# Attention beside a Mish layer on one core: strips and w1 pieces in the buffers of the gated rows, eleven power buffers in place of nine, and a new written order

## The chip, the core and the metric

The kernel runs on one core of a Trainium2 chip. The metric is the device time of one execution in microseconds (us), the median of several. Before the change it is 684.99 us (684.69 to 685.27 over three runs). One further execution was profiled; all rows of the profile below come from it.

The engines are called as the profile calls them: PE (matmul), PEld (its weight loads, which overlap it), DVE (VectorE), ACT (ScalarE), POOL (GpSimd) and SP (SyncE, whose queue issues nearly all DMAs).

## What is computed

```python
B, S, D = 1, 2048, 640            # of A and B; F = 1536
...
def _A_ref(x, wqkv, wo):
    B, S, D = x.shape
    H = 32; Dh = D // H
    qkv = (lambda x, *d: x.transpose(*d))((x @ wqkv).reshape(B, S, 3, H, Dh), 2, 0, 3, 1, 4)
    q, k, v = qkv[0], qkv[1], qkv[2]
    scale = Dh ** -0.5
    scores = jnp.einsum("bhqd,bhkd->bhqk", q, k) * scale
    p = _softmax(scores, axis=-1)
    o = jnp.einsum("bhqk,bhkd->bhqd", p, v)
    return (lambda x, *d: x.transpose(*d))(o, 0, 2, 1, 3).reshape(B, S, D) @ wo

def _B_ref(x, w1, b1, w2):
    h = jnp.einsum("bsd,df->bsf", x, w1) + b1
    sp = jnp.log1p(jnp.exp(-jnp.abs(h))) + jnp.where(h > 0, h, jnp.zeros_like(h))
    act = h * jnp.tanh(sp)
    return jnp.einsum("bsf,fd->bsd", act, w2)

x = A_x
g = _sigmoid((x * gate_w).sum(-1, keepdims=True))
a = _A_ref(x, A_wqkv, A_wo)
b = _B_ref(x, B_w1, B_b1, B_w2)
return g * a + (1 - g) * b
```

## The kernel before

**Tiling of the attention.** The 32 heads go in 8 sets of four, the 2048 queries in 4 columns of 512: 32 *groups* G of four heads and 512 queries. The keys of a group go in 16 *tiles* j of 128. One tile of one head is a *unit*: a score matmul (line 1074, contraction over 32 rows, so four heads can use four row groups of PE), 128 keys by 512 queries, into one PSUM bank of 512 f32. Banks 0 to 6 rotate, bank 7 is the accumulator `acc`. There are 32 x 16 x 4 = 2048 units.

**Two ways to the exponential.** For 345 of the 512 tiles ACT computes it (line 1092, one, two or three banks at a time) into a ring E of 18 slots. For the other 167 tiles DVE writes an integer approximation of a power of two (line 587), one instruction for each unit, into a buffer T of 4 x 512 bf16. Such a tile is then completed by POOL: two 64-bit integer additions over T (line 617) make shifted copies, in other buffers T or in place. Mostly the three versions go into the sum one by one (three P·V products, two of them with V scaled by a ratio, `VD`). Where a tile is taken with `two` = 1, DVE adds two versions first (line 641, 2048 elements), and two P·V products are enough. The buffers T are named by number, nine of them, 4 KB of each partition.

**P·V.** `emit_pv` (line 1109) multiplies four heads at once: four matmuls of 21 output columns side by side, 512 wide, into `acc`. The 21st column of V is ones and gives the denominator. When a group's last product is in, DVE transposes and divides (lines 1138 to 1152), and SP stores the result to DRAM.

**Chains.** All other products are *chains* (line 664): K, Q and V from x, h = x·w1, Mish·w2, and attention rows times wo. A piece of a chain is one contraction step: four matmuls of 32 output columns side by side, 512, 320, 240 or 81 wide. Q and K are made strip by strip (128 of their columns), each strip of weights loaded into one of two buffers for Q and two for K (`ws0_0`, `ws0_1`, `ws1_0`, `ws1_1`, `load_strip`); w1 comes in 24 pieces into two buffers (`w1t0`, `w1t1`, `load_w1`). Late in the kernel the attention rows come back transposed into two buffers `od0` and `od1` (`load_o`) to be multiplied by wo and gated. Mish itself is done by ACT in two instructions of 12288 elements (line 872), each between two loads of an activation table.

**The written order.** No scheduler moves anything: the string `ORDER` at the top of the file lists every step, and each engine and queue runs its own steps in that order, waiting on semaphores where data or a buffer is not ready. The letters: `S n,k` n score matmuls into banks from k on for ACT; `x n` one exp over n banks; `d G,k,two` takes a tile for the powers with buffer T number k; `D G,j,r,k` one score matmul of such a tile into bank k; `y n` the n-th waiting DVE instruction; `p n,k` the n-th waiting POOL addition, into buffer T number k (-1: in place); `V j,i` one P·V product of four matmuls; `C i,k` begins chain i in bank k and `F` emits a piece of it; `H` is four matmuls with zero weights (line 1124), which keep PE occupied; `m` is a Mish; `q`, `k`, `l`, `b`, `o` issue loads on SP.

Below, a *column group* is four matmuls side by side, as in `V`, `F` or `H`, and a *score run* is a stretch of score matmuls (`S`, `D`) with no column group between them.

Of the kernel before, what the change touches and what calls it, by code (L numbers as in the profile page):

```python
# [9 lines left out]
P = 128  # L10
# [3 lines left out]
BF16 = mybir.dt.bfloat16  # L14
# [17 lines left out]
V15,2 V15,1 x3 y59 l3 y60 x2 D1,12,0,5 y61 C19,6 S3,2 F F F F F F V3,-1 S2,0 D1,14,3,5 F d2,6,0 F F F x3 y62
V4,-1 S3,2 x2 l4 y63 p7,7 y64 q3 x1 x2 C21,2 V5,-1 V14,0 D1,13,3,6 S2,0 D2,15,0,5 F F F F p8,8 y65 y66 x2
D1,13,2,6 S2,3 l5 y67 V14,1 F x2 D1,12,3,5 S2,0 y68 p9,3 V14,2 V13,0 V6,-1 x2 y69 D1,12,2,6 S3,2 p10,1 y70 x1
l6 x2 C20,2 V7,-1 V13,1 d3,7,0 D1,12,1,5 S2,0 y71 x2 F F F F F F F F F D2,15,3,6 S3,3 F V12,0 V13,2 V8,-1
p11,3 y72 x3 l7 p12,8 y73 V12,1 S2,0 D2,15,1,6 y74 y75 x2 C22,2 V9,-1 F F D2,14,0,3 S2,4 F F F F D2,15,2,6
S2,0 F F F F y76 x2 l8 y77 x2 y78 S2,3 y79 x2 C23,6 D2,14,3,5 V12,2 F F V10,-1 D2,14,1,0 S2,1 F V11,-1 F y80
p13,3 d2,2,1 y81 x2 l9 y82 S2,3 D2,13,0,5 F F F F F S2,0 D2,14,2,2 F p14,0 x2 y84 x2 y83 y85 V15,2 S2,4
D2,13,3,3 V15,1 V0,-1 D2,13,1,2 S2,0 p15,8 x2 e0 p16,3 x2 y86 y87 y89 y90 e2 V1,-1 V15,0 C24,2 V14,0 V14,1
S2,3 D2,12,0,5 F F S2,0 D2,13,2,6 F F x2 y91 x2 D2,12,3,5 S2,3 d2,1,0 x2 y92 y93 p17,8 V2,-1 d3,0,0 F S2,0  # L40
D2,12,1,6 V3,-1 V13,0 V14,2 y94 x2 p18,5 y95 D2,11,0,4 S2,2 x2 C25,5 V13,1 F S2,0 D2,12,2,6 F F y96 y88 y97 x2
D2,11,3,4 S2,2 F F p19,4 y98 x2 S2,0 D2,11,1,6 y99 x2 y101 V4,-1 V13,2 S2,2 d3,3,0 C26,5 D3,15,0,4 F F F S2,0
D2,11,2,6 F V6,-1 y102 x2 S2,2 D3,15,3,4 F V5,-1 y100 x2 y103 y105 x2 p20,-1 q4 S2,0 V12,0 V7,-1 x2 y104
d3,8,0 p21,6 D3,14,0,6 S2,2 D3,14,3,5 V11,0 V12,1 y106 x2 S2,0 D3,15,1,4 p22,5 y107 x2 y108 V11,1 C27,5 V8,-1
D3,13,0,6 S2,2 F F F F F D3,15,2,4 S2,0 F F F F F y109 x2 y110 k1 x2 D3,13,3,6 S2,2 x2 y111 d3,6,0 y113 p23,2
y112 V11,2 V9,-1 S2,0 D3,14,1,4 V10,-1 C29,6 x2 d3,4,0 y114 F F S2,2 D3,12,0,5 F F p24,1 y115 x2 D3,14,2,4
S2,0 V15,0 F y116 x2 d4,5,0 y117 y118 y119 S2,2 D3,12,3,5 V15,1 V0,-1 p25,7 x2 S2,0 D3,13,1,4 y121 y122 V14,0
V15,2 D3,11,0,6 S2,2 V14,1 V1,-1 x2 p26,2 y123 x2 D3,13,2,5 D3,12,1,4 S2,0 y120 y124 x2 V14,2 V2,-1 C28,6 F F
F F F F F q5 y125 S2,2 D3,11,3,5 p27,2 S2,0 y126 x2 F F F p28,1 y127 x2 y128 v1,0 V3,-1 V13,1 V13,0 C30,6 S3,2
D3,10,0,5 F F F F F x1 x2 y130 y131 y129 y132 D3,10,3,5 S3,0 x1 d4,2,0 x2 C34,0 d4,0,0 V4,-1 V13,2 V5,-1 S2,3  # L50
D3,12,2,6 F F F y133 y134 x2 D4,15,0,5 S2,1 p29,7 y135 F F x2 y136 p30,3 V12,0 S2,3 D3,11,1,6 V6,-1 V12,1 x2
y137 S3,0 D3,11,2,5 V12,2 x1 y138 S2,3 D3,10,2,6 x2 y139 C31,0 d4,1,0 V7,-1 F v2,0 F F d5,7,0 p31,8 x2 S2,1
D3,10,1,6 D4,14,0,5 q6 p32,3 x2 V11,0 F S2,3 F V8,-1 V11,1 y143 y142 p33,6 x2 y144 D4,15,1,6 S2,1 D4,13,0,5
V10,0 V11,2 p34,8 y145 x2 S2,3 D4,15,2,0 y146 x2 y147 C32,5 V9,-1 V10,1 D4,14,1,6 S2,1 F V10,2 y148 x2 S2,3
D4,15,3,0 F F S2,1 D4,13,1,6 F F y149 x2 y150 x2 p35,6 S2,3 D4,14,2,0 V0,-1 V15,0 V1,-1 y151 y152 y154 x2 S2,1
D4,12,0,6 p36,3 x2 y155 y153 C33,5 F d4,4,0 V2,-1 F S2,3 D4,14,3,0 x2 V15,2 V15,1 S2,1 D4,12,1,6 F F F x2 y141
y157 y140 p37,8 D4,13,2,0 S2,3 V3,-1 V14,0 y158 y160 y159 x2 S2,1 D4,11,0,6 p38,5 y161 y156 x2 C35,0 V14,1
V4,-1 D4,13,3,5 S2,3 F F F y162 x2 d5,6,0 D4,11,1,6 S2,1 F F p39,3 y163 x2 S2,3 D4,12,2,5 y164 V5,-1 V14,2
p40,8 x2 S2,1 D5,15,0,6 y165 V6,-1 V13,1 y166 x2 D4,12,3,0 S3,3 y167 C36,6 V13,0 F F F D4,11,2,2 S2,0 F F x3
p41,5 y168 x2 p42,3 d5,2,0 y169 V13,2 C37,2 S3,3 F F S2,0 D4,11,3,6 V12,1 F F x3 x2 y170 p43,0 D5,15,1,5 S2,3  # L60
F V12,2 V11,0 V7,-1 x2 y171 y172 p44,8 S2,5 D5,15,3,0 D5,15,2,1 V9,-1 V11,1 S3,2 V10,-1 V12,0 V8,-1 V11,2 x2
y173 y174 x1 p45,5 y175 D5,14,0,6 S3,0 C38,5 F F F F F y177 p46,8 x2 x3 y176 y178 S2,3 V0,-1 V15,1 C39,0 V15,0
D5,14,1,6 S2,1 D5,13,0,5 x2 y179 y180 x2 d6,3,0 F F F F F y181 S2,3 D5,14,2,6 y182 x2 S2,1 x2 D5,13,1,5 V1,-1
d5,4,0 C40,0 V2,-1 V15,2 F y183 y184 D5,14,3,6 S2,3 d7,5,0 F F x2 D5,12,0,5 S2,1 y185 y186 F F p47,7 x2 y187
V3,-1 S2,3 C41,5 D5,13,2,6 V14,0 F p48,1 d6,0,0 x2 y188 D5,12,1,0 S2,1 F F D5,13,3,6 S2,3 F F y189 y190 x2
S2,0 D6,15,0,2 V4,-1 V14,1 V14,2 y191 p49,8 x2 y192 S3,3 D5,12,3,6 p50,6 y193 x2 V5,-1 V13,0 D5,12,2,2 S2,0 x3
y194 V6,-1 V13,1 V13,2 C42,6 F D6,14,0,5 S3,2 p51,7 F F F V12,0 q7 q8 d6,1,0 y195 x2 p52,6 x3 D6,15,2,5 S2,0
# [12 lines left out]
p66,1 D7,13,1,6 S2,4 F F F y242 x2 S2,1 D7,13,3,0 V2,-1 V14,0 k2 k3 p68,4 y243 x2 S2,4 D7,13,2,6 V14,1 V15,2  # L80
y244 y245 x2 D7,12,0,3 p69,8 d8,1,0 y246 C52,6 S3,0 V3,-1 F F F F F x1 x2 y248 D7,12,3,0 S3,3 V14,2 V4,-1
C53,6 x1 d7,3,0 x2 F F F d8,4,0 S2,1 D7,12,1,3 F F y249 y247 p70,-1 x2 y250 S2,4 D7,11,0,0 V5,-1 V13,0 y251
d8,8,0 x2 D7,12,2,3 S2,1 y252 x2 C54,6 V6,-1 V13,1 F y253 S2,4 D7,11,3,0 F D7,11,1,1 S2,2 F F F y254 p71,7 x2
# [226 lines left out]
def kernel(  # L310
# [15 lines left out]
    H = 32  # L326
# [1071 lines left out]
```

## Time and profile before

| | |
|---|---|
| median of the runs | 684.99 us |
| the profiled execution | 685.22 us |
| its span, first to last instruction | 683.3 us |
| around the span | 1.9 us |
| granted TensorE clock | 1.000 |
| POOL busy | 354.2 us (52%) |
| HBM read, written | 22.29 MB, 12.78 MB |

The busy shares of 40 equal slices of the span, in tenths, read:

```
PE   8999999999999999999999999999999999999997
DVE  5689988898989889989878988999998988898896
ACT  6999999999999999999999999999999999999996
POOL 5045446454454535565545654456645655466543
```

Each digit is one slice of 17 us. A busy PE is not yet a PE at its peak: the profile gives each matmul a modelled end, and matmuls that run side by side or behind each other overlap in it. How fast PE moves on is read from the starts of its rows in the timeline, not from durations.

### The profile page before, as it was taken

The numbers are of one execution on the slowest core, as the hardware profiler recorded it, in microseconds if no ns is written. First come the engines' busy times: TensorE is split into PE (matmuls) and PEld (weight loads), VectorE is DVE, ScalarE is ACT, GpSimd is POOL, SyncE is SP. The second block draws the span as 40 slices with busy tenths as digits, with TensorE's granted clock in tenths as the row PEclk, the third lists the DMA queues.
The fourth block names the chain that finished last, engine by engine and source line by source line (L and its number), as shares of the span: only waits on it lengthen the run. The fifth ranks groups of instructions, "written<-read, shape, count | busy, mean of one in ns | idle before, by whom it ended". The sixth has DMA issues, their size and how long they took to land.

```text
span 683.3 us, 24544 instructions
## 1 busy us (share of the span) xinstructions
PE 674.1 (99%) x10379; PEld 234.7 (34%) x10379; DVE 594.2 (87%) x1027; ACT 667.3 (98%) x693; POOL 354.2 (52%) x349
## 2 busy tenths in 40 slices
PE   8999999999999999999999999999999999999997
PEld 4433233323323443333333223222243333333334
DVE  5689988898989879989878988999998988898896
ACT  6999999999999999999999999999999999999996
POOL 5045446454454535565545654456645655466543
PEclk9999999999999999999999999999999999999999
DMA  8454312212312211111231223321332121131221
GB/s 170 115 95 131 81 33 49 57 38 60 92 25 53 45 48 36 26 35 34 42 93 37 42 54 72 64 50 39 56 93 59 20 48 30 42 67 34 59 86 60
DMA packets 128542, 40.47 MB, mean 59 GB/s; under 512 B 94960, under 2 KB 127872, under 8 KB 128432
## 3 DMA queue, kind: packets, MB, share of 16 engines
q1 hardware_dynamic: 126032, 38.29, 25.3%
q8 instruction: 81, 1.33, 0.8%
q10 hardware_dynamic: 2400, 0.62, 0.4%
q14 instruction: 29, 0.24, 0.1%
HBM read 22.29 MB, written 12.78 MB: 51 GB/s over the span
## 4 chain that ended last, share of the span: by engine, by line
PE 81%; ACT 13%; issue 2%; DVE 2%; DMA 1%; POOL 0%; SPq 0%; ACTq 0%; POOLq 0%
PE Sp L1109 27%; PE Sp L1074 27%; PE Sp L664 26%; ACT E L1092 11%; ACT big L872 2%; DVE T L587 1%; DMA wf<-in_A_wqkv_dram 1%; PE Sp L1337 0%; DVE VD L569 0%; DMA q_dram<-st 0%; PE Sp L1218 0%; PE Sp L1124 0%; ACT L1092 0%; DVE ot L973 0%; POOL T L617 0%
## 5 line engine op out<-in xcount | busy, mean ns | idle before, releaser
L1092 ACT ACTIVATE E<-Sp 128x1024 bf16<-128x1024 f32 (+2 forms) x675 | 635.2, 1116 | 5.5 <-PE Sp L1074 4.3
L617 POOL INT64_ADD T<-T x334 | 344.3, 1042 | 315.5 <-DVE T L587 237.6
L587 DVE TENSOR_SCALAR T<-Sp 128x512 int16<-128x512 f32 x668 | 441.0, 683 | 59.4 <-PE Sp L1074 49.4
L1074 PE MATMUL Sp<-qT,kT 32*128 32x512 bf16 x2048 | 258.3, 384 | 3.4 <-ACT E L1092 1.1
L1074 PEld LDWEIGHTS <-kT 32*128 32x128 bf16 x2048 | 69.0, 91 | 244.7 <-issue 240.3
L1109 PE MATMUL Sp<-E,VA 128*21 128x512 bf16 x1380 | 130.5, 382 | 0.1
L1109 PE MATMUL Sp<-T,VD 128*21 128x512 bf16 x1312 | 119.6, 382 | 0.1
L664 PE MATMUL Sp<-w_sb,big 128*32 128x320 bf16 x1536 | 73.6, 302 | 0.0
L664 PE MATMUL Sp<-xT,w1t 128*32 128x512 bf16 x960 | 73.1, 383 | 0.0
L1109 PEld LDWEIGHTS <-VA 128*21 128x21 bf16 x2048 | 44.1, 90 | 58.9 <-issue 50.4
L1109 PE MATMUL Sp<-T,VA 128*21 128x512 bf16 x668 | 64.0, 382 | 0.0
L664 PE MATMUL Sp<-xT,ws 128*32 128x512 bf16 x720 | 52.9, 382 | 0.0
L1109 PEld LDWEIGHTS <-VD 128*21 128x21 bf16 x1312 | 31.0, 90 | 38.0 <-issue 30.9
L664 PEld LDWEIGHTS <-big 128*32 128x32 bf16 x1536 | 33.0, 95 | 29.0 <-issue 21.6
L851 DVE TENSOR_SCALAR big<-Sp,b1f 128x512 bf16<-128x512 f32 x48 | 35.6, 741 | 1.9 <-PE Sp L664 1.2
L664 PE MATMUL Sp<-wv,xT 128*32 128x81 bf16 (+2 forms) x960 | 31.6, 257 | 0.1
L664 PEld LDWEIGHTS <-w1t 128*32 128x32 bf16 x960 | 20.2, 95 | 26.0 <-issue 18.8
L664 PE MATMUL Sp<-wo_sb,od 128*32 128x320 bf16 (+1 forms) x608 | 27.2, 301 | 0.1
L753 DVE CAST st<-Sp 128x512 bf16<-128x512 f32 x36 | 24.6, 683 | 2.9 <-PE Sp L664 1.9
L1138 DVE STREAM_TRANSPOSE T<-Sp 128x512 f32<-128x512 f32 x32 | 22.7, 709 | 2.3 <-PE Sp L1109 2.2
L664 PEld LDWEIGHTS <-xT 128*32 128x32 bf16 x960 | 19.4, 96 | 10.8 <-issue 7.9
L664 PEld LDWEIGHTS <-ws 128*32 128x32 bf16 x720 | 15.5, 95 | 19.1 <-issue 12.1
(76 smaller groups left out, 191.8 us busy)
## 6 DMA issues: line engine op xcount, KB each, us to landing
w1t<-in_B_w_dram SPq DMA_DIRECT2D x24, 320.0 KB
q_dram<-st SPq DMA_DIRECT2D x20, 128.0 KB
b_dram<-bt SPq DMA_DIRECT2D x16, 160.0 KB
bl<-b_dram SPq DMA_DIRECT2D x16, 160.0 KB
qT<-q_dram SPq DMA_DIRECT2D x124, 20.0 KB
o_dram<-T SPq DMA_DIRECT2D x120, 20.0 KB
out_dram<-ot SPq DMA_DIRECT2D x15, 160.0 KB
kT<-k_dram SPq DMA_DIRECT2D x28, 80.0 KB
```

The source lines that it names most:

```text
L587: nc.vector.tensor_scalar(out=dst.bitcast(I16), in0=src, scalar1=inv_sqrt_dh * LOG2E * 128.0, scalar2=127.0 * 128.0 + (BETA2 if two else B ...
L617: nc.gpsimd.int64_add(dst[:, :].bitcast(I64), src[:, :].bitcast(I64), n * 0x0001000100010001)
L664: nc.tensor.matmul(out_[k : k + 32], lhsT=lhsT[:, k : k + 32], rhs=rhs, tile_position=(0, k), **kw)
L753: nc.vector.tensor_copy(out=res["st"][:, :], in_=ps[:, :])
L851: nc.vector.tensor_scalar(out=big[:, pair_of(c, ft), (ft % 2) * QC : (ft % 2 + 1) * QC], in0=ps[:, :], scalar1=b1f[:, ft : ft + 1], scalar ...
L872: nc.scalar.activation(v, v, ACT.Mish)
L1074: nc.tensor.matmul(ps_cols, lhsT=kT[p][32 * t_ : 32 * t_ + 32, j * P : (j + 1) * P], rhs=qT[G][32 * t_ : 32 * t_ + 32, :], tile_position=( ...
L1092: nc.scalar.activation(E[:, x : x + n, :], allb[:, k0 : k0 + n, :], ACT.Exp, scale=inv_sqrt_dh,)
L1109: nc.tensor.matmul(acc[32 * t_ : 32 * t_ + DH + 1, :], lhsT=lhsT, rhs=rhs, start=(pv_done[G] == 0), stop=(pv_done[G] == pv_total[G] - 1), ...
L1138: nc.vector.transpose(out=st["T1"][:, :, :].rearrange("p b r -> p (b r)"), in_=acc[:, :])
```

## The change

The four strip buffers become one tile `strip_all` that takes the place of `od0`, and the two buffers for w1 become one tile `w1_all` in the place of `od1`. Every strip and piece has its own part of them, in the same double-buffered manner as before. Only the last Q strip, (0, 4), which is needed when `od0` is in use, keeps a buffer of its own, `ws`.

```diff
+    strip_all = work.tile([P, 4, KT, P], BF16, tag="od0", name="ws")
     w1t = {}
+    w1_all = work.tile([P, 2, KT, 2 * P], BF16, tag="od1", name="w1t")
...
     def load_strip(kind, i, eng):
-        t = work.tile([P, KT, P], BF16, tag=f"ws{kind}_{i % 2}", name="ws")
+        if (kind, i) == (0, 4):
+            t = work.tile([P, KT, P], BF16, tag="ws", name="ws")
+        else:
+            t = strip_all[:, 2 * kind + i % 2]
         c0 = kind * (D + HF) + i * P
         eng.dma_start(out=t[:, :, :], in_=wrows[:, :, c0 : c0 + P])
...
     def load_w1(k):
-            w1t[k] = work.tile([P, KT, W1N * P], BF16, tag=f"w1t{k % 2}", name="w1t")
+            w1t[k] = w1_all[:, k % 2]
```

Of each partition this frees four strips of 1,280 bytes and two pieces of 2,560 bytes, less the 1,280 bytes of `ws`: 8,960 bytes. Two more buffers T (4,096 bytes each), numbers 9 and 10, take them. The line numbers behind the edit are 5 higher in the changed file.

The string `ORDER` is another one throughout (the whole string is replaced). Counted letter by letter in the two strings:

| | before | after |
|---|---|---|
| score matmuls (`S`, `D`) | 2048 | 2048 |
| score runs | 642 | 630 |
| score runs in which a row group comes twice | 8 | 12 |
| `V`, of four matmuls each | 840 | 833 |
| tiles of powers (`d`); with `two` = 1 | 167; 6 | 167; 13 |
| `F`, pieces of chains | 1220 | 1220 |
| `H`, of four matmuls each | 6 | 3 |
| `x` over 1, 2, 3 banks | 32, 581, 62 | 79, 598, 35 |
| `x` in all | 675 | 712 |
| units of exp on ACT | 1380 | 1380 |
| `D` (one DVE power each) | 668 | 668 |
| `p` (POOL additions); in place | 334; 9 | 334; 14 |
| numbers of buffers T | 0 to 8 | 0 to 10 |

A line of the new order, as an example of how densely it is packed (part of group 29):

```
y912 p304,5 x2 V10,-1 S2,5 D29,12,0,3 y913 y914 x2 C164,2 D29,12,3,4 S2,0 F F F F x2
```

More of the change, by code (lines that the diff above doesn't have):

```diff
@@ L80 @@
[L80 to L83, printed above, removed]
-y255 x2 p72,6 S2,4 D8,15,0,0 V7,-1 V12,0 d9,5,0 y256 x2 S2,1 D7,11,2,3 y257 V8,-1 V12,2 S3,4 D8,14,0,0 y258 x2
@@ new lines @@
+D15,13,3,0 x2 y486 y488 C100,1 S3,2 x3 F F F F F y487 p151,0 D15,12,1,0 S2,5 F F F x2 y489 y490 S2,2
+D15,12,3,4 y491 y492 F F V14,0 x2 p152,3 S2,5 D15,12,2,0 d16,4,1 F F V15,0 y493 x2 D15,11,0,4 S2,2 V15,2
+p153,1 V12,0 d15,6,1 x2 y494 y495 S2,5 D15,11,1,0 v5,0 V14,2 V0,-1 y496 x2 p154,2 D15,10,0,4 D15,11,3,3 S2,1
+y499 V13,0 V14,1 x2 D15,11,2,0 S2,5 y500 V2,-1 V1,-1 x2 y501 S2,1 D15,10,3,4 V15,1 V3,-1 y502 x2 p155,9
+D15,10,1,3 S2,5 D15,10,2,0 V11,0 V13,2 y503 x2 d17,5,0 D16,15,0,4 S2,1 y504 V12,1 V4,-1 x2 y505 D16,15,1,3
@@ new lines @@
+V8,-1 V10,2 S2,0 D21,14,1,4 y664 x2 d22,3,0 y665 p215,6 C123,5 V9,-1 V10,1 S2,2 D21,14,0,6 F d21,4,0 F y667
+y666 x2 S2,0 D21,14,2,4 p216,9 F F F x2 y669 S2,2 V15,0 y668 y670 x2 D21,13,1,6 D21,13,2,4 S2,0 y672 x2 y673
+V15,1 V0,-1 C124,6 V15,2 S2,2 D21,14,3,5 V1,-1 F x2 y674 S2,0 D21,12,1,4 F F y671 x2 y675 p217,10 S2,2
+D21,13,0,5 F F y676 x2 D21,12,2,4 S2,0 p218,6 y677 V3,-1 V14,0 V2,-1 x2 d21,8,0 y678 S2,2 D21,12,0,5
+D21,13,3,6 V14,1 d22,2,0 V14,2 x2 y680 S2,0 D21,11,1,4 y679 p219,9 x2 y681 V4,-1 C125,5 V13,0 S2,2 D21,12,3,6
@@ new lines @@
+V13,0 F F F x2 y838 p278,1 S2,0 D26,11,1,5 x2 y839 F F F D26,12,3,4 S2,2 F F F F D26,11,2,5 S2,0 F F V13,2
+y840 x2 p279,10 y841 x2 S2,3 D26,11,0,2 y842 V13,1 V4,-1 p280,5 x2 y843 d28,8,0 D27,15,1,6 S2,0 D27,15,2,5
+V12,0 V5,-1 y844 x2 D26,11,3,2 S2,3 y845 V12,1 V6,-1 x2 y846 D27,14,1,6 S2,0 V7,-1 V12,2 y847 x2 p281,4
+D27,15,0,2 y848 d27,9,0 C151,6 S3,3 V11,0 x1 p282,1 x2 F F F F F F D27,15,3,3 S3,0 F F F F F F y849 x1 x2
+D27,14,2,0 S3,3 p283,2 q30 y850 V8,-1 V11,1 y851 x1 D27,14,0,6 d27,5,0 p284,3 x2 y852 S2,1 d28,10,0 C152,0
@@ L297 @@
+S3,2 D31,11,3,6 V6,-1 y993 x3 V12,2 V7,-1 D31,11,1,5 y994 C178,6 S2,0 F F F F x2 p333,5 S3,2 C179,5 F F F F F
+x2 V8,-1 V11,0 p334,3 y995 y996 b15 x1 S2,0 x2 S2,2 C180,6 F F F F C181,5 F F F F x2 y997 y998 C182,4 F F
+V11,1 V9,-1 V11,2 V10,-1 F F C183,2 F F F F y999 y1000 y1002 y1001 y1003
 """
```

531 lines of the change are left out of this document (259 added, 272 removed).

## Prediction

> **What bounds the kernel now.** I read the page first, for the busy shares and the chain of waits.
>
> ```profile
> span 683.3 us, 24544 instructions
> PE 674.1 (99%) x10379; PEld 234.7 (34%) x10379; DVE 594.2 (87%) x1027; ACT 667.3 (98%) x693; POOL 354.2 (52%) x349
> PE 81%; ACT 13%; issue 2%; DVE 2%; DMA 1%; POOL 0%; SPq 0%; ACTq 0%; POOLq 0%
> ```
>
> PE and ACT both look full. The chain that ended last runs through PE for 81% of the span, but a share says nothing of how tightly PE works, so the timeline of PE came next, in a plain stretch in the middle (columns: start, length, engine, line, what, count).
>
> ```profile
> 300.35 0.39 PE L1109 MATMUL Sp<-T,VA 128*21 128x512 bf16 x4
> 300.72 0.39 PE L1074 MATMUL Sp<-qT,kT 32*128 32x512 bf16 x3
> 301.04 0.61 PE L1109 MATMUL Sp<-T,VD 128*21 128x512 bf16 x8
> 301.48 0.39 PE L664 MATMUL Sp<-xT,ws 128*32 128x512 bf16 x4
> 301.80 0.39 PE L1074 MATMUL Sp<-qT,kT 32*128 32x512 bf16 x3
> ```
>
> Starts, not lengths: eight matmuls (two column groups) from 301.04 to 301.48 take 0.44 us, so a column group of 512 costs 0.22. The next one, from 301.48 to the score run at 301.80, takes 0.32: 0.10 more, because the tiling of PE changes. A score run takes 0.32 again (300.72 to 301.04). A score run therefore costs 0.32 + 0.10 = 0.42 us, whether it holds two, three or four matmuls on different row groups. Between these rows PE never rests. Third, the waits of PE (total us, times, longest).
>
> ```profile
> PE Sp L1074 <- ACT E L1092: 1.1, 1, 1.1
> PE Sp L1074 <- DVE T L587: 0.9, 2, 0.5
> ```
>
> These are the only waits for a bank that outlast the matmul before them. The one of 1.1 us is the first score run after a Mish. So PE sets the time, by the number of its column groups and score runs. Next, is ACT a second bound? The groups by shape (busy us, mean ns of one | idle before):
>
> ```profile
> L1092 ACT ACTIVATE E<-Sp 128x1024 bf16<-128x1024 f32 x581 | 552.6, 1097 | 4.6 <-PE Sp L1074 3.5 <-ACT E L1092 0.4 <-PE Sp L1109 0.2
> L1092 ACT ACTIVATE E<-Sp 128x1536 bf16<-128x1536 f32 x62 | 95.0, 1532 | 0.8 <-PE Sp L1074 0.8
> L872 ACT ACTIVATE big<-big 128x12288 bf16<-128x12288 bf16 x2 | 20.9, 10445 | 0.0
> L1092 ACT ACTIVATE E<-Sp 128x512 bf16<-128x512 f32 x32 | 20.8, 669 | 0.1
> L872 ACT ACT_TABLE_LOAD x2 | 2.6, 1283 | 0.0
> L1092 ACT ACT_TABLE_LOAD x2 | 2.6, 1283 | 0.0
> ```
>
> and ACT's timeline at both ends:
>
> ```profile
> 9.11 5.61 ACT L1092 ACTIVATE E<-Sp 128x1024 bf16<-128x1024 f32 x6 [1.18 <-PE Sp L1074]
> ...
> 675.95 1.07 ACT L967 ACTIVATE big<-Sp,g_t 128x320 bf16<-128x320 f32 x2 [1.25 <-PE Sp L664]
> ```
>
> Exps overlap. Six two-bank exps take 5.61 us, the last of them 1.10, so one follows another after (5.61 - 1.10) / 5 = 0.90 us. A bank more costs (1.532 - 0.669) / 2 = 0.43 us by the lengths, so an instruction costs some 0.05 beyond its banks; the banks are then (0.90 - 0.05) / 2 = 0.425 each. All exps at that pace are 1380 x 0.425 + 675 x 0.05 = 620 us. They have the stretch from 9.11 to 674.70 (675.95 less the wait of 1.25), less both Mish and the four table loads (20.9 + 2.6 + 2.6): 639.5 us. ACT has some 19 us to spare, hidden inside rows that look back to back.
>
> **The change, part by part, on PE.** The counts are those of the two written orders.
>
> Column groups: 7 fewer `V` and 3 fewer `H` are 10 fewer, at 0.22: -2.2 us. The 7 come from seven more tiles with two = 1.
>
> Score runs: the same 2048 matmuls in 630 runs in place of 642: 12 x 0.42 = -5.0 us.
>
> Runs in which a row group comes twice, four more. Such a run has two passes:
>
> ```profile
> 511.57 0.61 PE L1074 MATMUL Sp<-qT,kT 32*128 32x512 bf16 x5
> 512.11 0.46 PE L664 MATMUL Sp<-wo_sb,od 128*32 128x320 bf16 x8
> ```
>
> It takes 0.54 in place of 0.32, 0.22 more: 4 x 0.22 = +0.9. PE's own work falls by 2.2 + 5.0 - 0.9 = 6.3 us.
>
> **Banks that are written again sooner.** Fewer, longer runs leave less PE work between two writings of a bank, and the exp or power that empties it must fit in there. I walked both orders and added up the work between, at 0.42 for a run, 0.22 for a `V` and 0.18 for an average chain piece (an estimate from the 512- and 320-wide pieces). Before, the least is 1.07 us, at one place, and 1.15 elsewhere, and the rows above show two waits of PE for DVE, 0.9 us together. In the new order twelve places lie under 1.07: 1.04 once, 0.97 five times, 0.86 twice, 0.64 three times, and once 0 in the first Mish stretch. The example line is one of the 0.64. What they lack of 1.15 adds up to 4.3 us. Behind a waiting score matmul everything on PE queues, so such a wait is paid in full, except where PE would have waited anyway. The bounds are 0 and 4.3; nothing excludes either end; I take 2.0, about the middle, as the shortage is counted from the nearest place that costs nothing.
>
> **ACT.** 37 more instructions for the same banks. The nearest rows bound one by 0.05 (above) and 0.24 (two lone banks, 2 x 669, against one pair, 1097 ns): 1.9 to 8.9 us. I take 0.05, since at the pace of 0.90 the exps do overlap. ACT's spare 19 us shrink by 1.9 and by PE's 6.3 to some 11. So the 1.9 lie beside PE's work and count 0; with that cover gone they would be on the path.
>
> **Mish.** While ACT does a Mish (10.4 us and two table loads, 13.0 in all), PE lives on work laid by. The first stretch holds 54 column groups and 4 runs in place of 61 and 2: 7 x 0.22 - 2 x 0.42 = 0.7 us less to do. The second holds 56 groups and 6 runs in place of 52 and 3, some 2 us more, where before `H` filled in:
>
> ```profile
> 515.41 0.40 PE L1124 MATMUL Sp<-xT,zero_w 128*21 128x512 bf16 x4
> ...
> 516.07 0.39 PE L1124 MATMUL Sp<-xT,zero_w 128*21 128x512 bf16 x4
> ...
> 516.50 0.39 PE L1124 MATMUL Sp<-xT,zero_w 128*21 128x512 bf16 x4
> ```
>
> A loss of up to 0.7 against a gain of the same size: 0, within 0.7 either way.
>
> **DVE, POOL and the buffers.** Groups by shape again; the row of L641 is from the view of the tile T and has lengths as min/median/max in ns.
>
> ```profile
> L587 DVE TENSOR_SCALAR T<-Sp 128x512 int16<-128x512 f32 x668 | 441.0, 683 | 59.4 <-PE Sp L1074 49.4
> L617 POOL INT64_ADD T<-T x334 | 344.3, 1042 | 315.5 <-DVE T L587 237.6 <-PE Sp L1109 32.0 <-PE Sp L1074 23.8
> L641 DVE TENSOR_TENSOR T<-T x6: 1207/1214/1215, 72.5 to 267.1; 128x2048 bf16<-128x2048 bf16 x6
> L1109 PE MATMUL Sp<-T,VD 128*21 128x512 bf16 x1312 | 119.6, 382 | 0.1
> ```
>
> Seven more additions on DVE are 7 x 1.21 = 8.5 us against 683.3 - 594.2 = 89 idle; behind one of them a power can be 1.2 us late and its bank with it, so 0 to 8.5, and I take 0: the six of before made only POOL wait. Two more buffers T can spare POOL up to 32.0 + 23.8 us of waiting for PE (an old buffer still being read). PE's products from T sat idle for 0.1 us, so POOL is on nobody's path: 0, and no loss, since the additions stay 334. What the buffers buy is the freedom for the order, counted above.
>
> **Strips and pieces.** The same loads into other addresses; every part is still double-buffered, and in the new order `od0` is first loaded after the last strip in it was read, at 70% of PE's instructions against 61%: 0. If the shared tile made a load or a product wait for a neighbour part, cover is gone (a rival below).
>
> **Sum.** -6.3 + 2.0 = -4.3 us on the span of 683.3, or 679.0. The profiled execution took 685.22, that is 0.23 above the median of 684.99; from the median I forecast 680.7 us.
>
> **The rivals.**
>
> *All of PE's saving arrives:* the short places cost nothing, since ACT and DVE are ahead there. 684.99 - 6.3 = 678.7. For it: waits of 0.9 us in all before. Against: those had 1.15 us.
>
> *It cancels:* the short places cost their 4.3, and a few powers behind longer DVE additions the remaining 2: 685.0.
>
> *ACT is the bound:* the saving on PE becomes PE's waiting, and 37 x 0.05 comes on top: 684.99 + 1.9 = 686.9. For it: busy 98%, and 13% of the chain. Against: 19 us to spare. The Trainium skill's Perfetto Trace Analysis, section "Identifying the Most-Contended Engine", speaks for it: it says that matmul busy time is no fair measure of PE and that occupancy is one for ACT, so by that page's rule ACT at 98% would be the engine to look at. The starts in the rows above differ from it on both engines.
>
> *Slower, by banks:* not only those twelve places wait. Banks with less than 1.5 us until a next score for ACT, or 1.05 for DVE, are 64 in the new order against 30, by the same walk. If each of the 34 more cost 0.3 us, that is 10.2, and 684.99 - 6.3 + 10.2 = 688.9. It decides from 0.23 us each on, where the 34 outweigh 6.3 by the 1.4 us that can be told from no change. Against: the 30 of before cost next to nothing.
>
> *The shared tile adds waits, so the change doesn't do what it says:*
>
> ```profile
> ws<-in_A_wqkv_dram SPq DMA_DIRECT2D x9, 160.0 KB
> ...
> SPq L781 <- DMA q_dram<-st: 13.6, 12, 2.1
> ```
>
> Eight strip loads, each waited for in full at up to 2.1 us (the longest wait for a landing of 128 KB), would add 16.8: 695.5. For it: one tile where there were four. Against: each use reads or writes one part.
>
> **How the numbers follow.** Forecast 0.47; all of the saving 0.16; cancelling 0.12; ACT 0.10; banks 0.11; shared tile 0.04. The forecast's own range is 678.4 to 683.0 (short places between 0 and 4.3). For 8 in 10 the range goes down to 677.5 (the saving and 0.7 from Mish, and half a microsecond), and up to 687.5, past the ACT case; left out are the last two cases. A run of this kernel can tell 0.2%, some 1.4 us, from no change. Faster: 0.47 + 0.16, and a part of the cancelling case that ends below, 0.64; same 0.12; slower the rest, 0.24.
>
> **What would show it.** Right: starts of PE rows at the same 0.22 and 0.42, fewer by the counts; a span near 679; PE's waits for ACT and DVE a little above 2 us; ACT still waiting for PE; POOL waiting less for PE. Wrong: long waits of PE at the short places, above all in group 15 and in the last groups; exps at 0.90 without a pause over whole groups while PE waits (ACT); PE or SP waiting for landings of strips.

## The result and the profile after

| | before | after |
|---|---|---|
| median | 685.12 us (684.69 to 688.25, 6 runs) | 689.75 us (688.73 to 691.00, 6 runs) |
| ratio, 95% interval | | 1.0059 (1.0045 to 1.0074) |
| profiled execution, its span | 685.22, 683.3 us | 690.21, 688.3 us |

The changed kernel is slower, by 5.0 us in the spans. Forecast was 680.7 us, with 687.5 as the upper end. The page after, its head, busy shares and chain of waits:

```profile
span 688.3 us, 24517 instructions
...
PE 673.3 (98%) x10339; PEld 236.9 (34%) x10339; DVE 601.9 (87%) x1034; ACT 669.3 (97%) x730; POOL 358.6 (52%) x349
...
PE 77%; ACT 16%; DVE 3%; issue 3%; POOL 0%; ACTq 0%; DVEq 0%
```

PE has 40 matmuls fewer (ten column groups), as counted. Its share of the chain is down from 81 to 77%, that of ACT up from 13 to 16%. ACT's groups by shape (busy us, mean ns of one | idle before):

```profile
L1097 ACT ACTIVATE E<-Sp 128x1024 bf16<-128x1024 f32 x598 | 578.5, 1113 | 7.3 <-PE Sp L1079 6.3 <-ACT E L1097 0.5 <-PE Sp L1114 0.2
L1097 ACT ACTIVATE E<-Sp 128x512 bf16<-128x512 f32 x79 | 57.9, 733 | 1.3 <-PE Sp L1079 1.2
L1097 ACT ACTIVATE E<-Sp 128x1536 bf16<-128x1536 f32 x35 | 54.7, 1564 | 0.6 <-PE Sp L1079 0.6
```

The waits of PE (us in total, times, longest):

```profile
PE Sp L1079 <- DVE T L592: 2.0, 3, 1.1
PE Sp L1114 <- issue: 1.9, 1, 1.9
PE Sp L1079 <- ACT E L1097: 1.5, 5, 0.4
```

The second row is new: PE waited 1.9 us for nothing that the profile shows. The other two were 0.9 and 1.1 before. These rows hold a few us, no more, and they leave out what PE waits while an earlier matmul still counts as running. So I measured by starts: how much later each score matmul starts than it does after the same kind of predecessor elsewhere (0.32 us after a 512-wide column group). Added up over all places above 0.08 us, that is 7.7 us in 35 places before and 14.2 us in 50 after.

Where the 5.0 us arise is told by two instants that both kernels share, the starts of an early score matmul, number 131, and of the last one (number 2048):

```
us from the span's start        before   after   difference
score matmul 131                 56.71   59.18    +2.5
from there to the last one      615.92  618.56    +2.6
from there to the end            10.71   10.59    -0.1
```

So there are two losses: one in the first 57 us, and one in the long middle. In three other runs of the old order (below: shared buffers, no `H`, the edits of the start) the middle was 615.85 to 615.90, so it is steady to 0.1 us. The first mark is less so: it lies at 56.6 to 57.7 us in the profiles of four kernels with the old order and the old loads (before, shared buffers, no `H`, 30 `V` fewer), and at 57.4 in another kernel with the start of the changed one (the loosened order). The +2.5 is that of two executions.

*The start.* PE's timeline (start, length, engine, line, what, count, idle before):

```profile
24.75 0.40 PE L1079 MATMUL Sp<-qT,kT 32*128 32x512 bf16 x4
25.08 0.39 PE L1114 MATMUL Sp<-E,VA 128*21 128x512 bf16 x1
27.34 0.61 PE L1114 MATMUL Sp<-E,VA 128*21 128x512 bf16 x7 [1.88 <-issue]
```

One matmul of a column group runs at 25.08, its three neighbours 2.26 us later; the profile names nothing that they wait for ("issue"). The windows of that stretch (busy us and count of PE, PEld, DVE, ACT, POOL; granted clock; DMA share; GB/s):

```profile
24.00:25.00 1.00, 1.00 (x20) 0.31 (x12) 0.61 (x2) 1.00 (x2) 0.00 (x0) 1.00 0.95 263
...
26.00:27.00 1.00, 0.00 (x0) 0.00 (x0) 0.83 (x2) 0.29 (x1) 0.00 (x0) 1.00 0.13 30
27.00:28.00 1.00, 0.66 (x13) 0.33 (x14) 0.00 (x0) 0.00 (x0) 0.00 (x0) 1.00 0.05 12
28.00:29.00 1.00, 1.00 (x12) 0.11 (x5) 0.00 (x0) 0.00 (x0) 0.00 (x0) 0.55 0.21 48
29.00:30.00 1.00, 1.00 (x15) 0.45 (x16) 0.00 (x0) 0.84 (x1) 0.00 (x0) 0.50 0.12 30
30.00:31.00 1.00, 1.00 (x16) 0.16 (x4) 0.00 (x0) 0.68 (x2) 0.00 (x0) 0.50 0.42 138
31.00:32.00 1.00, 1.00 (x13) 0.23 (x13) 0.63 (x1) 0.20 (x1) 0.00 (x0) 0.74 0.16 41
```

After the stop the clock is at about half from 28.0 to 31.5 us, and PE shows a busy 1.00 all the while: another 1.7 us by the clock (0.45 + 0.50 + 0.50 + 0.26). The kernel with the loosened order (below) has the same start, and in its profile a stop of 1.90 us there is not followed by half a clock; its score matmul 131 starts 1.8 us earlier (57.37), 0.4 of it by the shorter stop, so the halved clock costs some 1.4 here.

The 800 KB load of `wv` fills the DMA engines until 25 us. The queue that carries instructions (q8) brings blocks of 16 KB; in this trace one was sent at 18.24 and the next at 24.79, in that burst; before they were sent at 20.01 and 24.02. Over the sixteen profiles of this study, the third block in the trace (here that of 24.79) went out at 24.79 us or later in six, and each of the six has a stop named "issue" behind it, of 0.8 to 1.9 us; it went out at 24.43 or earlier in the other ten, and none of them has one there. Two of the six have the old order and the old loads (without `H`, and with more exps), so the stop is not the new order's alone. ACT has no exp for 2.87 us there, since its scores are not made.

*The middle.* One row of ACT's timeline, in the group of the example line:

```profile
628.05 9.28 ACT L1097 ACTIVATE E<-Sp 128x1024 bf16<-128x1024 f32 x10
```

Ten exps start within 9.28 - 1.1 = 8.2 us, one every 0.91. By the starts, most pairs follow each other after 0.903 us, never less; a single bank after 0.477 and three after 1.330. With these three floors the middle splits into what ACT must spend on its exps, what it lets pass between them, and the rest (both Mish with their table loads, and small operations):

```
            exps of 2 / 1 / 3 banks   floor   let pass   rest    middle
before        544 /  29 / 51          572.9     13.7     29.3    615.9
after         552 /  73 / 32          575.8     13.1     29.4    618.6
```

413 of the 624 exps of before, and 431 of 657 after, start within 5 ns of their floor. ACT has 2.95 us more to do in the middle (33 more instructions of 0.05, and three more banks of 0.43, which before lay outside the two marks), and lets 0.65 less pass. That is 2.3 of the +2.6 without any word of PE, although PE has less work there (0.1 is in the rest, and the three terms of after fall 0.3 short of its middle). Without marks, over all exps of the run: ACT's floors are 1.91 us more; what it lets pass is 4.29 more in the first 60 us and 0.53 less behind them; the first exp starts 0.36 earlier, and what follows the last one is 0.31 shorter. That makes the 5.0. Whether this is cause or coincidence was for the runs to say.

### The profile page after: what moved, and what is told of

It reads as the page before. It is cut to its first block, busy times and chain, and to the rows that moved or that the text cites. A ratio compares the mean times of both kernels' runs of the same rounds, so it can differ in the third digit from the quotient of the medians.

```text
span 688.3 us, 24517 instructions
## 1 busy us (share of the span) xinstructions
PE 673.3 (98%) x10339; PEld 236.9 (34%) x10339; DVE 601.9 (87%) x1034; ACT 669.3 (97%) x730; POOL 358.6 (52%) x349
## 4 chain that ended last, share of the span: by engine, by line
PE 77%; ACT 16%; DVE 3%; issue 3%; POOL 0%; ACTq 0%; DVEq 0%
PE Sp L1079 26%; PE Sp L1114 26%; PE Sp L669 25%; ACT E L1097 12%; ACT big L877 3%; DVE T L592 2%; PE Sp L521 0%; ACT L1097 0%; PE Sp L1342 0%; DVE ot L978 0%; PE Sp L1223 0%; DVE T L646 0%; ACT L877 0%; DVE VD L574 0%; DVE T L1143 0%
## 5 line engine op out<-in xcount | busy, mean ns | idle before, releaser
L622 POOL INT64_ADD T<-T x334 | 348.8, 1055 | 314.7 <-DVE T L592 246.0
L1079 PEld LDWEIGHTS <-kT 32*128 32x128 bf16 x2048 | 70.5, 91 | 244.2 <-issue 239.5
L669 PE MATMUL Sp<-xT,w1t 128*32 128x512 bf16 x960 | 71.7, 383 | 0.3 <-DVE big L856 0.3
L669 PE MATMUL Sp<-w_sb,big 128*32 128x320 bf16 x1536 | 71.2, 301 | 0.2
L1114 PEld LDWEIGHTS <-VA 128*21 128x21 bf16 x2048 | 45.6, 90 | 62.1 <-issue 52.7
L669 PEld LDWEIGHTS <-big 128*32 128x32 bf16 x1536 | 34.5, 96 | 26.4 <-issue 19.2
```

The source lines that it names most:

```text
L622: nc.gpsimd.int64_add(dst[:, :].bitcast(I64), src[:, :].bitcast(I64), n * 0x0001000100010001)
L669: nc.tensor.matmul(out_[k : k + 32], lhsT=lhsT[:, k : k + 32], rhs=rhs, tile_position=(0, k), **kw)
L1079: nc.tensor.matmul(ps_cols, lhsT=kT[p][32 * t_ : 32 * t_ + 32, j * P : (j + 1) * P], rhs=qT[G][32 * t_ : 32 * t_ + 32, :], tile_position=( ...
L1114: nc.tensor.matmul(acc[32 * t_ : 32 * t_ + DH + 1, :], lhsT=lhsT, rhs=rhs, start=(pv_done[G] == 0), stop=(pv_done[G] == pv_total[G] - 1), ...
```

## The experiments

Each kernel was run beside the kernel before, whose medians in the four series were 685.78, 685.83, 685.64 and 686.06 us; comparisons with it are within a series.

### The start

**The wv load in two** (in the changed kernel):

```diff
+            if i == 0:
+                nc.sync.dma_start(
+                    out=wv[:, :, 4 * HF : D], in_=wrows[:, :, 2 * D + 4 * HF : 3 * D]
+                )
...
-    nc.sync.dma_start(out=wv[:, :, :], in_=wrows[:, :, 2 * D : 3 * D])
+    nc.sync.dma_start(out=wv[:, :, HF : 4 * HF], in_=wrows[:, :, 2 * D + HF : 2 * D + 4 * HF])
```

> The changed kernel; only the 800 KB load of wv is cut: columns 80 to 319 (300 KB) stay at their place, columns 320 to 639 are issued with the late Q strip, columns 0 to 79 (which no product reads) are left out. Refill theory: PE's next block of instructions was fetched late, behind that load, so PE stood for 1.9 us at 25 us and its clock was then halved for some 3.4 us, together 3.6 to 3.8 us; so no such idle row, clock 1.000, and 686.0 us (685.2 to 687.0). Rival, banks alone: the start has nothing to do with the load; idle row and clock as before, 689.75 within 0.7.

Measured: 687.98 us, ratio 1.0032 (1.0019 to 1.0044). The profiled execution took 690.10, the longest of the twelve, and shows no gain: score matmul 131 starts at 59.00 us (59.18 without the edit). The stop at 25 us is gone and the clock is 1.00 up to 37 us. But PE's timeline has a new wait at 36.85 us, the halved clock now stands behind that one, and SP's queue shows why (its rows: start, length, line, what, count):

```profile
36.85 0.39 PE L1083 MATMUL Sp<-qT,kT 32*128 32x512 bf16 x3 [2.09 <-POOL T L626]
```

```profile
38.00:39.00 1.00, 1.00 (x19) 0.29 (x15) 0.11 (x1) 0.70 (x1) 0.00 (x0) 0.50 0.38 96
39.00:40.00 1.00, 1.00 (x23) 0.53 (x15) 0.58 (x1) 0.99 (x1) 0.00 (x0) 0.50 1.06 236
```

```profile
24.64 5.78 SPq L729 DMA_DIRECT2D k_dram<-kT  x12
30.52 1.25 SPq L765 DMA_DIRECT2D q_dram<-st  x1
31.86 1.55 SPq L729 DMA_DIRECT2D k_dram<-kT  x4
33.51 0.34 SPq L765 DMA_DIRECT2D q_dram<-st  x1
33.95 0.38 SPq L765 DMA_DIRECT2D k_dram<-st  x1
34.43 2.56 SPq L790 DMA_DIRECT2D qT<-q_dram  x7
```

The row names POOL, one of whose additions happens to end at 36.81. But the matmul also waits for a reload of `qT` from `q_dram` that was issued at 35.18 and landed at 36.72, and in the kernel with the shorter powers (below) the profile puts the same wait down to that reload:

```profile
PE Sp L1082 <- DMA qT<-q_dram: 1.8, 1, 1.8
```

The reload stands behind two stores of `q_dram`, which stand behind sixteen stores of the upper rows of K. By the medians 1.8 us came back, about half of what the refill theory expected. That this wait took the rest is seen in the profiled execution alone, where it took all.

**The wv load twice** (in the kernel before, a second load of the same 800 KB into a part of the tile `big` that nothing uses by then):

```diff
     nc.sync.dma_start(out=wv[:, :, :], in_=wrows[:, :, 2 * D : 3 * D])
+    nc.sync.dma_start(
+        out=flat[:, 8192 : 8192 + KT * D].rearrange("p (k d) -> p k d", d=D),
+        in_=wrows[:, :, 2 * D : 3 * D],
+    )
```

> The kernel before, with a second load of 800 KB into a part of the tile big that nothing uses by then, issued right behind the load of wv. Refill theory: the fetch of PE's instructions at 24.0 us now comes behind the longer burst; PE stands for 1 to 3 us near 25 to 28 us for want of instructions, its clock falls below 1.000, and the time is 687 to 690 us. Rival, the load is harmless to PE: 685.1 within 0.7, clock 1.000.

Measured: 687.83 us, ratio 1.0028 (1.0013 to 1.0042). The wait and the clock, from the views of waits and of windows:

```profile
PE Sp L664 <- issue: 1.6, 1, 1.6
```

```profile
31.00:32.00 1.00, 1.00 (x11) 0.11 (x3) 0.03 (x1) 1.00 (x2) 0.00 (x0) 0.50 0.14 36
32.00:33.00 1.00, 1.00 (x15) 0.35 (x16) 0.69 (x1) 0.91 (x2) 0.00 (x0) 0.50 0.34 111
```

In the profiled execution the kernel before gets the same stop and the same halved clock once a longer burst stands there; its middle is 0.5 us shorter (615.42). The instruction block went out at 26.61 in place of 24.02. The halved clock does not come each time: in seven of the twelve executions the mean granted clock was 0.999 or 1.000.

**The wv load in two and the K stores later** (in the changed kernel; the sixteen stores moved to the end of the loads):

```diff
+                for c in range(NQC):
+                    store_top(c)
...
-            return [(lambda x=x: copy(*x)) for x in parts], lambda: store_top(c)
+            return [(lambda x=x: copy(*x)) for x in parts], None
```

> The changed kernel with the wv load in two (the third that the first V columns need at its old place, the other columns after the other loads), and the sixteen stores of k_dram's upper rows moved from the chains to the end of the loads, so that no such store stands ahead of q_dram's stores on SP's queue. Theory A (two limits at the start: PE's instruction block behind the wv load, then the strips of Q for group 1 behind those stores): the first score matmuls of group 1 no longer wait (2.1 us with the split alone) and start near 35 us, the clock in 28 to 33 us is near 1, and the time is 685.5 to 686.5, 3.3 to 4.2 us under the changed kernel's 689.75. Theory B (the start is worth only what the split alone brought, and what stands behind it is not SP's queue): 687.5 to 688.5, with a wait of about 2 us still ahead of group 1's scores.

Measured: 687.61 us, ratio 1.0029 (1.0020 to 1.0038). Group 1's scores now start at 34.75 us in place of 38.22, and score matmul 131 at 55.70, a microsecond ahead of the kernel before. Yet only 2.1 us came back, and the whole is still 1.8 us slower than before, and 2.7 slower than the old order with the same two edits (next): the middle is 619.5. Theory A's account of the start holds and its forecast of the time does not.

**The same two edits in the kernel before**, as a control.

> The kernel before with the same two edits at the start (wv in two, k_dram's upper stores later). In its trace PE does not stand for its instructions there and group 1's scores wait 0.2 us only, so theory A (the edits help because the changed order has a stall to be removed) expects 684.6 to 685.4, no change. Theory B (the edits are a gain for any order) expects 682 to 683.

Measured: 684.88 us, ratio 0.9982 (0.9973 to 0.9992), middle 615.90. A gain of about 1 us at the most, in the range of theory A; this is the fastest complete kernel of the study.

**Column groups that add zero, in the first Mish** (five `H` in the kernel with both edits of the start):

```diff
-q13 y352 D10,11,2,5 D10,11,1,4 y355 p104,-1 y353 D10,11,3,4
-y354 y356 D11,15,0,6 C81,5
+q13 y352 D10,11,2,5 D10,11,1,4 H y355 H p104,-1 H y353 H D10,11,3,4
+y354 H y356 D11,15,0,6 C81,5
```

> The changed kernel with wv in two and k_dram's upper stores later (a_split_tops), and five H (column groups that add zero) in the places where PE stands idle for 0.3 to 1.5 us in the first Mish. Theory A (PE's idling of some 2 us there makes the clock fall to half for 3 to 4 us afterwards, 0.50 at 242 to 245 us in the profile of a_split_tops): no halved clock after the first Mish, and 1.5 to 2 us less than a_split_tops, 685.6 to 686.2. Theory B (the clock falls there for another reason, or costs nothing since ACT is behind): within 0.6 us of a_split_tops's 687.6, or slower by the H.

Measured: 687.35 us, ratio 1.0022 (1.0011 to 1.0032), 0.3 us under the kernel without them (0.5 by the ratios, since the two stand in different series). First the windows without, then with the five `H`:

```profile
242.00:243.00 1.00, 1.00 (x24) 0.70 (x19) 0.63 (x2) 0.99 (x2) 0.42 (x1) 0.50 0.20 65
243.00:244.00 1.00, 1.00 (x20) 0.48 (x12) 1.00 (x2) 1.00 (x2) 0.00 (x0) 0.50 0.00 0
244.00:245.00 1.00, 1.00 (x16) 0.31 (x16) 0.44 (x2) 0.53 (x2) 0.55 (x1) 0.50 0.00 0
```

```profile
242.00:243.00 1.00, 1.00 (x36) 0.90 (x32) 1.00 (x3) 0.98 (x2) 0.56 (x1) 1.00 0.39 131
243.00:244.00 1.00, 1.00 (x36) 0.72 (x25) 0.96 (x3) 0.99 (x2) 0.48 (x1) 1.00 0.00 0
244.00:245.00 1.00, 0.57 (x15) 0.28 (x12) 1.00 (x1) 1.00 (x2) 0.00 (x0) 1.00 0.00 0
```

The clock follows PE's idling, as theory A said; the price falls short of it. In the profile without the `H`, ACT's table load after the Mish ends at 242.45 us, and two of its next four exps wait 0.47 and 0.20 us for PE. Three of the eleven executions without the `H` had a mean clock of 1.000 and took 686.8 to 687.0 us, the other eight (0.996 and 0.997) 687.5 to 688.0: the drop goes with 0.5 to 1.3 us. With the `H` the clock was 0.999 or 1.000 in all nine and the time 686.6 to 687.8, so five `H` give back part of what they win.

### The parts of the change that cost nothing

**The shared buffers with the old order** (the diff's code, the string of before).

> The kernel before with its own order, but strips and w1 pieces in the shared tiles in place of od0 and od1 (nine buffers of powers used, as before). If the buffers cost nothing and the order does it all: 685.1 within 0.7, PE's waits as before (1.1 us for ACT, 0.9 for DVE). If the shared tile adds waits for neighbour parts: over 687, with PE or SP waiting for a strip or a piece.

Measured: 685.49 us, ratio 0.9995 (0.9985 to 1.0006). Strips and pieces in shared buffers are free; it is the order that costs. (PE waits 1.5 us for `qT` near 36 us in this profile, for the reload named above and not for a strip.)

**The kernel before without its six `H`.**

> The kernel before without its six H (24 matmuls with zero weights), which leaves out no part of the computation. If the heaters hold the clock and the new order lost it by having fewer: clock below 1.000 and 686 to 689 us. If they only fill time in which PE waits (refill theory says the clock fell for another reason): clock 1.000, 685.1 within 0.7.

Measured: 685.73 us, ratio 1.0000 (0.9989 to 1.0011). So `H` are not needed in the old order; in the new one only the five above were tried.

### The middle

**The order loosened** at eight of the longest waits of score matmuls (column groups `F` and `V` that stood behind such a matmul now stand ahead of it), for example

```diff
-... C164,2 D29,12,3,4 S2,0 F F F F x2 y907 y915 S2,5
+... C164,2 D29,12,3,4 F F F F S2,0 x2 y907 y915 S2,5
```

> The changed kernel with its order loosened at eight places where a score matmul waited over 0.35 us for its bank: column groups that stood behind it (F, V) now stand ahead of it; the same work otherwise, the start untouched. The waits at those places sum to about 5 us of the 14.2 us that the changed kernel's score matmuls wait in all. Theory A (banks written again too soon cost their wait in full): these waits shrink to under 1.5 us in sum, and the time falls by 3 to 4 us, to about 686. Theory B (the waits move on to the next place, since ACT's rate sets them): the sum of score waits stays within 1.5 us of 14 and the time within 1 us of 689.75.

Measured: 690.35 us, ratio 1.0060 (1.0046 to 1.0075). The score matmuls wait 13.1 us in all, against 14.2. The wait that stood at 621 us moved to the next score run (0.55 at 622.7), those at 336 and 521 grew from 0.27 to 0.73 and from 0.23 to 0.77, and the middle is 620.8. The wait at 517 us went over to a column group, which that sum leaves out (before the edit this row read 0.7, 3, 0.2):

```profile
PE Sp L669 <- DVE T L592: 1.3, 3, 0.9
```

Theory B: the waits move on. **With the edits of the start as well:**

> The edits of the two kernels before it together. If the start and the banks are two separate causes, the two gains add: 682 to 683.5, under the kernel before (685.1) by 0.2 to 0.4 per cent. If they are one cause seen twice, it is no better than the better of the two, about 686.

Measured: 688.84 us, ratio 1.0038 (1.0025 to 1.0051), no better than the edits of the start alone. The two gains do not add, since the second is none.

**Exps over 448 of 512 columns**, in the changed kernel and in the kernel before:

```diff
-            E[:, x : x + n, :], allb[:, k0 : k0 + n, :], ACT.Exp, scale=inv_sqrt_dh,
+            E[:, x : x + n, 0:448], allb[:, k0 : k0 + n, 0:448], ACT.Exp, scale=inv_sqrt_dh,
```

> The changed kernel with exps over 448 of 512 columns of each bank (the other columns of the exps are zero, so the output differs); PE, DVE, POOL and the order as in the changed kernel. A pair should follow another after some 0.79 us in place of 0.90. Theory A (in the places where score matmuls wait, ACT is already at its own pace of 0.90, so its pace over a stretch sets the wait): the score waits of 14.2 us fall by 5 or more, and the time by 4 to 7 us, to 683 to 686. Theory B (what counts is the single place, a bank written again too soon, with ACT otherwise ahead): each of some 15 waits for an exp shrinks by the 0.13 us by which a pair is shorter, 2 us in all, 687 to 688. The start costs the same in both.

> The kernel before with exps over 448 of 512 columns, the control to the same edit in the changed kernel. Its score matmuls wait 7.7 us in all, 2 of them for an exp outright. If PE alone bounds it, as the prediction said, 683.5 to 685, at most 1.5 us under 685.1. If ACT's pace bounds it too, 680 to 682.

Measured: 681.98 us, ratio 0.9939 (0.9920 to 0.9957) in the changed kernel; 680.95, ratio 0.9930 (0.9914 to 0.9946) in the kernel before, 4.7 us under it. The largest group of ACT, in the one and in the other:

```profile
L1098 ACT ACTIVATE E<-Sp 128x896 bf16<-128x896 f32 x598 | 529.5, 917 | 28.2 <-PE Sp L1080 17.8 <-PE Sp L1115 0.8 <-ACT E L1098 0.3
```

```profile
L1093 ACT ACTIVATE E<-Sp 128x896 bf16<-128x896 f32 x581 | 512.1, 917 | 27.3 <-PE Sp L1075 18.5 <-ACT E L1093 1.2
```

Now ACT waits for PE, 18 us where it was 6.3 and 3.5. A pair follows another after 0.80 us at the least, so ACT's floor in the middle fell by some 68 us, but the middle by 5.2 only (before) and by 7.2 (changed): in the kernel before PE is the next bound, 1% below. The time of the changed kernel fell by 7.8 us, more than theory A's 4 to 7; its score waits fell by some 4, not by 5 or more. What stayed of them is told by PE's waits there, for ACT and for DVE (1.5 and 2.0 in the changed kernel as it was):

```profile
PE Sp L1080 <- DVE T L593: 2.2, 4, 1.1
PE Sp L1080 <- ACT E L1098: 0.2, 1, 0.2
```

By the starts, five of the longest waits behind score matmul 131 are as long as with full exps: 1.51, 0.89, 0.64, 0.59 and 0.59 us. They do not come from ACT's pace in the exps (three of them lie within a Mish). Together with its later start and a clock of 0.50 from 242 to 245 us after the first Mish they are of the size of what PE saves, and the changed kernel is not ahead even here; what each of them costs was not told apart. That the kernel before gains 4.7 us from faster exps alone is what the prediction's theory did not allow.

**Powers over 448 of 512 columns** in the changed kernel, the same cut for DVE.

> The changed kernel with powers over 448 of 512 columns (the other columns zero; the output differs); all else as in the changed kernel. A power should take 0.53 to 0.60 us of DVE in place of 0.60 to 0.68. If DVE's pace sets the waits at D places (six of the thirteen longest waits), the score waits fall by 2 to 4 us and the time by 2 to 4, to 686 to 688. If ACT alone sets them, the time stays within 1 us of 689.75.

Measured: 689.65 us, ratio 1.0062 (1.0038 to 1.0086), no change. A power took 619 ns in place of 683. The start of its profile was 0.8 us later and its middle 0.6 shorter (eleven memsets on POOL come in at the start; the stop at 25 us is gone there and the wait for `qT` is 1.8 us). DVE's pace over a stretch is not what costs. But of the five waits above it shortens none by more than 0.09 us, so this run says little of their price.

**Less work for PE alone**: the kernel before without 30 column groups `V`.

```diff
+            if pv_n[0] in SKIP:
+                e_at.pop((G, j, t_), None)
+                continue
...
```

> The kernel before with 30 column groups V left out, spread evenly over the run, each standing behind another column group (so the output differs): PE has 30 x 0.22 = 6.6 us less to do, ACT, DVE and POOL the same. Theory PE (PE sets the time and ACT has some 18 us to spare): 6 to 6.6 us less than the kernel before in the same call. Theory ACT (exps follow each other at their own pace over most of the run, and PE only waits more): 0 to 2 us less, with the idle of ACT in front of exps smaller by about as much.

Measured: 684.59 us, ratio 0.9984 (0.9968 to 0.9999): 1.5 us of 6.6, and 1.0 in the middle (614.9). The busy shares and ACT's largest group:

```profile
PE 671.8 (98%) x10259; PEld 236.2 (35%) x10259; DVE 593.2 (87%) x1027; ACT 666.5 (98%) x693; POOL 354.1 (52%) x349
...
L1094 ACT ACTIVATE E<-Sp 128x1024 bf16<-128x1024 f32 x581 | 552.7, 1105 | 4.5 <-PE Sp L1076 3.9 <-ACT E L1094 0.4
```

120 matmuls fewer, and PE is busy for 2.3 us less only: it stands behind ACT.

**More instructions for ACT alone**: the kernel before with 116 of its pairs cut in two.

```diff
+        ex_n[0] += n == 2
+        step = 1 if n == 2 and ex_n[0] % 5 == 0 else n
+        for h in range(0, n, step):
...
```

> The kernel before with every fifth exp of two banks split into two of one bank, the same banks, values and order: 116 more instructions on ACT, 116 x (2 x 0.477 - 0.903) = 5.9 us more at ACT's pace; PE, DVE and POOL the same. Theory ACT: 4 to 6 us slower than the kernel before in the same call. Theory PE: hidden in ACT's 18 us to spare, 0 to 1.5 us slower.

Measured: 690.53 us, ratio 1.0067 (1.0051 to 1.0082), 4.5 us slower. Its profiled execution was the longest of the six (692.63) and shows a stop at the start too (1.4 us of "issue" at 28 us, and a late `qT`), so I read the middle alone: 620.5, +4.6. ACT's account of the two runs beside that of before:

```
                floor   let pass   rest    middle
before          572.9     13.7     29.3    615.9
b_less_pe       572.9     12.8     29.3    614.9
b_more_exps     578.5     12.5     29.5    620.5
```

Work taken from PE leaves ACT's floor as it is, and 1.0 of 6.6 us arrives; work given to ACT arrives at 4.6 of 5.6. Theory ACT, in both.

## Why the prediction was wrong, step by step

*"So PE sets the time, by the number of its column groups and score runs."* This step failed. PE's counts and cadences were right: by its starts, PE's own work fell by some 6 us, against 6.3 forecast. But a saving on PE alone arrives at 1.0 to 1.5 of 6.6. I had found ACT's pace of 0.90 and then taken the sum of what it lets pass, 19 us, as cover. That sum was nearly right (16.5 us by the starts of all exps) and was no cover: two thirds of the exps already stood at their floor, and the 14 us of the middle come in short gaps, of which 30 products less on PE closed 0.9. The rows of waits had also misled: they showed 2.0 us for a bank where score matmuls started 7.7 us late. The sign that the prediction named for ACT, exps at 0.90 without a pause, is the row at 628.05.

*"The 1.9 lie beside PE's work and count 0."* Failed by the same error. The size was right: 712 exps in their new shapes cost 624.2 us at their floors, where 675 cost 622.4, 1.9 more over the whole run. That is most of the 2.7 us by which the new order is slower where both have the two edits of the start (687.61 against 684.88). The rival "ACT is the bound", 686.9 at a chance of 0.10, was the case in the middle; with the 2.5 us of the start it makes 689.4, and 689.75 was measured. That it comes so near is in part luck, since the start differs by over 1 us between executions. The rule beside it, from the Trainium skill's Perfetto Trace Analysis, section "Identifying the Most-Contended Engine", was the better guide: by occupancy ACT at 98% was the engine to look at, and the runs agree with it (4.7 us from 12.5% less exp, 1.5 from less PE work).

*The start had no term.* 2.5 us: PE stops for its instructions behind the `wv` burst and is then granted half a clock. I had looked at what the change does to loads it touches, not at what an earlier or later PE meets in the loads it leaves alone. That size and place of the load can make and unmake the stop was shown on both kernels; they are not all, since the stop also came in two kernels with the old order and the old loads. That the late block of instructions is the link is inferred from the times of the blocks, which part the sixteen profiles without exception.

*"Banks that are written again sooner", +2.0.* The places were right: the "once 0" in the first Mish waits 1.5 us, the example line 0.67, group 15 0.46. The meaning was not. Score matmuls wait 6.5 us more than before, over three times the term. With faster exps about 4 us of their waits go, so these came from ACT at its floor, and the longest stay, so those are the places' own. Neither kind sets the time while ACT does, and loosening the places moved the waits.

*Mish, 0 within 0.7.* PE's idling in the first one grew from 1.1 to 2.0 us (windows from 241 to 247 us in both profiles), about the 0.7 that I counted, and ACT's time over both Mish is the same to 0.1 us: right at 0. That the idling can halve the clock for three microseconds was missed, at up to about 1 us in the kernel with both edits of the start.

*DVE, POOL, buffers, strips at 0.* Right as far as the time goes: shorter powers changed nothing, and the shared buffers measure 0.9995. One sum was off: the lower end of the forecast's own range, 684.99 - 6.3, is 678.7 and not 678.4.

What stays open: what the places that wait as long with shorter exps cost with ACT out of the way (the rows name DVE there); which of the moved instructions makes PE's block late in the new order, and whether an order with the old count of ACT instructions and the new PE counts would be faster; that was not tried.

## What to carry to other kernels

When two engines both look full, compare the start-to-start times of each with the shortest that the same shape ever shows: the engine most of whose instructions sit exactly at that floor is the first to suspect (here it set the time), and the slack that is left in a sum is not cover. The cheapest proof is a pair of runs on the old kernel, one that takes work from the one engine and one that gives work to the other. And a reordered start meets the old loads at other moments: look at which transfer PE's instructions, and the first reloads on a queue, will stand behind.

## What the runs showed of the hardware

- Near a burst of 800 KB PE can stand for 0.8 to 1.9 us with no wait on any semaphore in the trace: 1.9 us in the changed kernel, none with 300 KB there, 1.6 us when the kernel before loads it twice, none in its own profile. It stood in the six profiles whose block of instructions went out at 24.79 us or later, and in none of the ten where it went out by 24.43. That it stands for want of instructions is inferred from this.
- A stop of 2.26 us was followed by a clock of 0.50 to 0.55 for about 3.4 us. The Trainium skill's TensorE: Matmul & The Clock Gate, Part 1, states about that length for the window by which the clock is judged, and that it runs freely; these runs agree with the length, and show that idling of about 2 us can be enough and need not be: a stop of 1.90 us at the same place in the kernel with the loosened order was followed by a clock of 1.00. In the first Mish PE idled for 1.6 us within three (238 to 241 us) in the kernel with both edits of the start, and for 1.4 (241 to 244) in the changed kernel; the clock fell in the first profile and stayed at 1.00 in the second.
- An exp of one, two or three banks of 512 columns follows the one before it after 0.477, 0.903 and 1.330 us, to a few ns, though its row is 0.67 to 1.56 us long: 0.427 a bank and 0.05 an instruction.
